# A cast moved to ScalarE and a mask product cut in two at the start of a fused retention and MLP kernel

## The chip, the cores and the metric

The kernel runs on one core of one Trainium2 chip. The metric is the device time of one execution in microseconds (us), the median of several runs. The measured time is some 1.8 us longer than the span that the profile shows (214.87 against 213.1 us for the profiled run of the kernel before).

## The reference

A recurrent retention layer over 4 batches, 8 heads, 768 steps and a head size of 64, then a layer norm and an MLP (512 to 2048 to 512) with a residual:

```python
for t in range(S):
    state = gamma[None, :, None, None] * state + np.einsum('bhd,bhe->bhde', k[:, :, t], v[:, :, t])
    y[:, :, t] = scale * np.einsum('bhd,bhde->bhe', q[:, :, t], state)
...
mu, var = x.mean(-1), ((x - mu) ** 2).mean(-1)          # shortened
xn = (x - mu) / np.sqrt(var + 1e-06) * g_ln
out = x + np.maximum(xn @ w_ch1, 0.0) @ w_ch2
```

## The kernel before

The 768 steps are cut into chunks of 128, which gives 24 tiles of 128 rows. For each tile TensorE transposes k and q (tasks tk and tq), VectorE scales the transposed q (trq), TensorE multiplies q and k (pa), VectorE applies the decay mask (asb), TensorE multiplies with v (py, and pyS for the part that comes from the state; pd updates the state), VectorE takes the statistics and normalizes (xn), TensorE transposes (tx), ScalarE copies the result (xnt), and then come the MLP units (m1, with a relu by ScalarE or VectorE) and the second product (m2). For the first eight tiles an MLP unit is 16 matmuls, 0.89 us: one tile with one of the four chunks of w1.

The order of all this is not written down. Tasks are listed with an engine (or a choice of engines), an estimated duration, a rank and what they wait for; a planner in the kernel simulates them and fixes the order of each engine's instructions before the program is built. So a change of one entry can move instructions anywhere.

```python
def order(self):
    ...
    key = at + t["polite"], t["rank"], at      # the task that can start first, then by rank
    if best is None or key < best[0]:
        best = key, t, e
...
def c_mask(eng):
    nc.vector.tensor_tensor(
        out=mask, in0=vsc[:, 0, :].unsqueeze(2).to_broadcast([P, H, P]),
        in1=cm.unsqueeze(1).to_broadcast([P, H, P]), op=ALU.mult)
...
maskd = a(DVE, 1230, -50, c_mask, [vscd, tri])
...
# tile 0: loaded as fp32 by two hardware queues, and cast; the other tiles are cast by GpSimd's DMA
raw = a(ACT if kind == "q" else SP, 390, -200 + "kqv".index(kind), emit32, (),
        ("osb", kind), (), 0, {"k": 3400, "q": 4000, "v": 4800}[kind])
loaded[kind, j] = a({"k": {ACT: 620}, "q": {DVE: 490}, "v": {ACT: 620, DVE: 430}}[kind], 0, -60, emit,
                    [raw], takes, [("osb", kind)])
...
tk = a(PE, 230, r - 0.1, e_tk, [loaded["k", t], ident] + ([tq] if tq else []),
       ("tp", ("k", t)), [where["k", t]], follows=[pat] if t == 1 else [])
...
m = a(PE, 865, 500 + unit["1", g, ho], e_m1,
      [ex[t] for t in range(G0[g], G0[g] + n)] + [loaded["w1", ho // 4]],
      ("mm", key), [("xnt", hb)])
```

The loads after tile 0 are issued by GpSimd one after another: k, q and v of the next tiles with the chunks of w1 between them, then w2.

## Time and profile before

| | before |
|---|---|
| time, median of 3 | 214.69 us (214.67 to 214.78) |
| span in the profile | 213.1 us |
| TensorE busy | 203.6 us, 96% |
| VectorE, GpSimd, ScalarE busy | 57%, 42%, 38% |
| TensorE starts tk of tile 4, the seam | 23.39 us |
| TensorE ends its last matmul | 210.02 us |

From the page of the kernel before, the busy time of each engine and TensorE's share of 40 equal slices in tenths (9 is 90% or more):

```profile
PE 203.6 (96%) x1935; PEld 131.4 (62%) x1955; DVE 121.3 (57%) x235; ACT 80.8 (38%) x152; POOL 89.8 (42%) x105
...
PE   7769999999999999999999999999999999999994
```

The row of digits says where most of the idle time lies: in the first three slices (16 us), where TensorE waits for loads and for the chain of the first tiles, and in the last one. It says so roughly. The busy time holds 6.4 us of filler, matmuls on zeros (L650) that the planner puts into early gaps, so the early slices wait longer than their digits say; and a 9 can hide up to a tenth of 5.3 us, as in the fifth slice the wait of 0.44 us at the seam. From the start of tk4 at the seam to its last end TensorE is busy in 185.40 of 186.63 us, so after the seam there is nearly nothing to gain by a faster engine alone, while anything that makes TensorE wait there is felt.

### The profile page before, as it was taken

The numbers are of one execution on the slowest core, as the hardware profiler recorded it, in microseconds if no ns is written. First come the engines' busy times: TensorE is split into PE (matmuls) and PEld (weight loads), VectorE is DVE, ScalarE is ACT, GpSimd is POOL, SyncE is SP. The second block draws the span as 40 slices with busy tenths as digits, with TensorE's granted clock in tenths as the row PEclk, the third lists the DMA queues.
The fourth block names the chain that finished last, engine by engine and source line by source line (L and its number), as shares of the span: only waits on it lengthen the run. The fifth ranks groups of instructions, "written<-read, shape, count | busy, mean of one in ns | idle before, by whom it ended". The sixth has DMA issues, their size and how long they took to land.

```text
span 213.1 us, 4678 instructions
## 1 busy us (share of the span) xinstructions
PE 203.6 (96%) x1935; PEld 131.4 (62%) x1955; DVE 121.3 (57%) x235; ACT 80.8 (38%) x152; POOL 89.8 (42%) x105
## 2 busy tenths in 40 slices
PE   7769999999999999999999999999999999999994
PEld 2448899995476556777877785454544444444442
DVE  7688778961736989987872869793511111012121
ACT  4446655772042203645644353145640044430000
POOL 8988699826498395665834550000000000000000
PEclk9999999999999999999999999999999999999999
DMA  7999999999999999999999999820121111011212
GB/s 140 180 179 180 180 156 190 169 185 155 149 202 190 130 245 201 134 165 128 172 131 142 122 177 152 222 77 0 34 65 50 52 49 49 0 52 49 98 49 98
DMA packets 109382, 27.17 MB, mean 127 GB/s; under 512 B 102065, under 2 KB 106417, under 8 KB 109362
## 3 DMA queue, kind: packets, MB, share of 16 engines
q0 software_dynamic: 75984, 13.24, 87.8%
q1 hardware_dynamic: 32194, 13.31, 34.7%
q10 hardware_dynamic: 1184, 0.33, 0.7%
q8 instruction: 15, 0.25, 0.5%
q14 instruction: 5, 0.04, 0.1%
HBM read 27.27 MB, written 6.29 MB: 157 GB/s over the span
## 4 chain that ended last, share of the span: by engine, by line
PE 87%; DMA 8%; POOL 2%; issue 1%; DVE 0%; POOLq 0%
PE tp L626 39%; PE mm L589 37%; DMA ksb<-in_k_dram 5%; DMA w<-in_moe_w_ch_dram 3%; PE pa L443 3%; PE pd L512 2%; PE py L466 2%; PE py L462 2%; PE tp L542 1%; POOL k L342 0%; PE tp L403 0%; POOL qsb L342 0%; POOL v L342 0%; POOL w L350 0%; PE tp L411 0%
## 5 line engine op out<-in xcount | busy, mean ns | idle before, releaser
L589 PE MATMUL mm<-xnt,w 128*128 128x128 bf16 (+2 forms) x896 | 93.7, 257 | 0.0
L626 PE MATMUL tp<-w,h 128*128 128x512 bf16 (+2 forms) x381 | 86.7, 370 | 1.2 <-issue 0.3
L602 ACT ACTIVATE h<-mm 128x512 bf16<-128x512 f32 x88 | 52.5, 597 | 70.5 <-PE mm L589 59.6
L589 PEld LDWEIGHTS <-w 128*128 128x128 bf16 x896 | 65.7, 98 | 18.5
L626 PEld LDWEIGHTS <-h 128*128 128x128 bf16 x400 | 37.3, 98 | 38.8
L634 DVE SCALAR_TENSOR_TENSOR osb<-tp,rstd,x_all 128x512 f32<-128x512 f32 (+2 forms) x25 | 18.2, 728 | 55.3 <-PE tp L626 55.1
L450 DVE TENSOR_TENSOR asb<-pa,mask 128x1024 bf16<-128x1024 f32 x24 | 29.3, 1220 | 9.6 <-PE pa L443 9.4
L480 DVE BATCH_NORM_STATS2 bns<-py 128x6 f32<-128x512 f32 x24 | 16.7, 696 | 14.6 <-PE py L466 14.4
L499 POOL TENSOR_TENSOR vg<-vsb,vsc 128x512 bf16<-128x512 bf16 x16 | 17.2, 1073 | 13.3 <-DMA vsb<-in_v_dram 9.2
L486 ACT CAST x_all<-py 128x512 bf16<-128x512 f32 x24 | 14.0, 583 | 19.1 <-DVE xn L475 19.0
L342 POOL DMA_DIRECT2D qk<-in_k_dram x17 | 15.2, 893 | 12.3 <-DMA tr<-qk 9.9
L342 POOL DMA_DIRECT2D vsb<-in_v_dram x20 | 18.5, 923 | 1.2 <-DMA w<-in_moe_w_ch_dram 0.8
L475 DVE SCALAR_TENSOR_TENSOR xn<-py,mv,gb 128x512 bf16<-128x512 f32 x24 | 18.0, 751 | 0.9
L526 DVE TENSOR_TENSOR state<-pd,gch 64x256 bf16<-64x256 f32 x40 | 16.7, 417 | 0.3
L342 POOL DMA_DIRECT2D qk<-in_q_dram x17 | 15.2, 894 | 3.4 <-DMA w<-in_moe_w_ch_dram 3.4
L433 DVE TENSOR_TENSOR trq<-tr,qsc 128x512 bf16<-128x512 bf16 x17 | 7.9, 463 | 2.9 <-DMA tr<-qk 2.9
L564 ACT ACTIVATE rstd<-mv,epsb 128x1 f32<-128x1 f32 (+2 forms) x14 | 3.7, 289 | 11.8 <-DVE mv L481 11.8
L466 PEld LDWEIGHTS <-asb 128*128 128x128 bf16 x192 | 7.8, 98 | 0.3 <-DVE trq L416 0.3
L462 PEld LDWEIGHTS <-trq 128*128 128x128 bf16 x80 | 6.0, 98 | 3.2
L466 PE MATMUL py<-vsb,asb 128*128 128x64 bf16 x160 | 7.9, 193 | 0.0
L462 PE MATMUL py<-state,trq 128*128 128x128 bf16 x80 | 7.7, 219 | 0.1
L650 PE MATMUL mm<-zeros 128*128 128x512 bf16 (+1 forms) x24 | 6.4, 394 | 1.4 <-DVE zeros L221 1.2
(65 smaller groups left out, 108.4 us busy)
## 6 DMA issues: line engine op xcount, KB each, us to landing
out_dram<-osb SPq DMA_DIRECT2D x23, 256.0 KB, 4.0
w<-in_moe_w_ch_dram POOLq DMA_DIRECT2D x8, 512.0 KB, 10.3
vsb<-in_v_dram POOLq DMA_DIRECT2D x20, 128.0 KB, 8.8
qk<-in_k_dram POOLq DMA_DIRECT2D x17, 128.0 KB, 9.3
qk<-in_q_dram POOLq DMA_DIRECT2D x17, 128.0 KB, 9.9
qsb<-in_q_dram POOLq DMA_DIRECT2D x6, 128.0 KB, 8.7
k<-in_k_dram POOLq DMA_DIRECT2D x3, 128.0 KB, 7.4
v<-in_v_dram POOLq DMA_DIRECT2D x3, 128.0 KB, 9.0
```

Of the source, the lines that this page charges most:

```text
L342: nc.gpsimd.dma_start(out=tile_of(kind, j), in_=src)
L450: nc.vector.tensor_tensor(out=take("asb", t, [P, NPAIR, 2, P], BF16).rearrange("p i a t -> p a i t"), in0=held["pa", t], in1=mask.rearrang ...
L462: nc.tensor.matmul(py[:, 2 * i:2 * i + 2, :], lhsT=held["trq", t][:, i, :], rhs=held["pb", t][:, i, :], start=(mi == 0), stop=False)
L466: nc.tensor.matmul(py[:, h, :], lhsT=held["asb", t][:, h // 2, h % 2, :], rhs=tile_of("v", t)[:, h, :], start=(mi == 0), stop=(mi == n - 1))
L475: nc.vector.scalar_tensor_tensor(out=take("xn", t, [P, DM], BF16), in0=held["py", t].rearrange("p h d -> p (h d)"), scalar=mv[:, t, 0:1], ...
L480: nc.vector.bn_stats(out=bns[:, t, :], in_=held["py", t].rearrange("p h d -> p (h d)"))
L499: e.tensor_tensor(out=take("vg", j, [P, H, D], BF16), in0=tile_of("v", j), in1=vsc[:, cc, :].unsqueeze(2).to_broadcast([P, H, D]), op=ALU. ...
L526: nc.vector.tensor_tensor(out=held["pb", n][o, :, o], in0=held["pd", b][o, :, o], in1=gch[o, cc, :].unsqueeze(2).to_broadcast([D, NPAIR, D ...
L589: nc.tensor.matmul(p[:, j, :], lhsT=w1[:, ko, (ho + j) * P:(ho + j + 1) * P], rhs=held["xnt", hb][:, h0:h0 + n, ko, :], start=(ko == 0), s ...
L602: nc.scalar.activation(out=dst, in_=src, func=AF.Relu)
L626: nc.tensor.matmul(held[key], lhsT=held["h1", hb][:, ho, i * P:(i + 1) * P], rhs=w2[:, ho, cols], start=(ho == 0), stop=(ho == HO - 1))
L634: nc.vector.scalar_tensor_tensor(out=take("osb", key, [P, w], FP32), in0=held[key], scalar=rstd[:, t:t + 1], in1=x_all[:, t, cols], op0=AL ...
```

## The change

Its intent is to shorten the start. The cast of v goes to ScalarE, which is idle then (from 6.62 to 8.46 us in the trace before), so VectorE is free for the first scaled q; and the mask product is cut into two halves of heads, so the first half runs while q is still on its way. Estimates of landing times and of the setup were adjusted with it, for the planner.

```diff
-    def c_mask(eng):
+    def c_mask(eng, s):
+        n = s.stop - s.start
         nc.vector.tensor_tensor(
-            out=mask, in0=vsc[:, 0, :].unsqueeze(2).to_broadcast([P, H, P]),
-            in1=cm.unsqueeze(1).to_broadcast([P, H, P]), op=ALU.mult)
+            out=mask[:, s], in0=vsc[:, 0, s].unsqueeze(2).to_broadcast([P, n, P]),
+            in1=cm.unsqueeze(1).to_broadcast([P, n, P]), op=ALU.mult)
...
-    small = a(DVE, 1450, -100, c_small)
+    small = a(DVE, 1550, -100, c_small)
...
-    maskd = a(DVE, 1230, -50, c_mask, [vscd, tri])
+    maskd = a(DVE, 640, -50, lambda eng: c_mask(eng, slice(0, H // 2)), [vscd, tri])
+    maskd = a(DVE, 640, -45, lambda eng: c_mask(eng, slice(H // 2, H)), [maskd], at=5300)
...
-                        ("osb", kind), (), 0, {"k": 3400, "q": 4000, "v": 4800}[kind])
+                        ("osb", kind), (), 0, {"k": 3400, "q": 3800, "v": 5200}[kind])
...
-                loaded[kind, j] = a({..., "v": {ACT: 620, DVE: 430}}[kind], 0, -60, emit,
+                loaded[kind, j] = a({..., "v": {ACT: 620}}[kind], 0, -60, emit,
```

More of the change, by code (lines that the diff above doesn't have):

```diff
@@ L334, in emit @@
                              held["osb", kind].rearrange("p (h d) -> p h d", d=D))
-                loaded[kind, j] = a({"k": {ACT: 620}, "q": {DVE: 490}, "v": {ACT: 620, DVE: 430}}[kind], 0, -60, emit,
+                loaded[kind, j] = a({"k": {ACT: 620}, "q": {DVE: 490}, "v": {ACT: 620}}[kind], 0, -60, emit,
                                     [raw], takes, [("osb", kind)])
```

## The prediction

General statements that no run of this case shows are cut from the text below, at the marked places: on how the engines' queues run, on formulas for the time of an operation, on small DMA packets, on loads that no engine can hasten and on transposes behind stores. The times the forecast uses (1.23, 0.68 and 0.62 us) are read from the trace, and its sum came to +0.7, 215.4, of which 215.3 was taken. In the trace of the kernel before the stretches from 8 to 40 us move 156 to 206 GB/s, a little wider than the 174 to 206 said below.

> **What bounds the kernel now.** I read the page's busy shares first, then the chain of work that ended last, then the stretches, then the timeline of the first 44 us. TensorE is busy 96% of 213.1 us at full clock; nothing else is over 57%. The chain says where the other 4% lies:
>
> ```profile
> 4.19 7.25 DMA w<-in_moe_w_ch_dram
> ...
> 11.73 0.76 POOL w L350
> 12.66 10.68 DMA ksb<-in_k_dram
> 23.39 0.40 PE tp L403 x4
> 23.78 0.89 PE mm L589 x16
> ...
> 197.95 12.09 PE tp L626 x71
> 210.06 0.35 DVE osb L634
> ```
>
> Columns: start, length, what. Up to 23.39 us the chain is DMA: loads by GpSimd, one after another, down to k of tile 4 (the L403 transpose is "tk4" below; tasks are numbered in their order on TensorE). From 23.39 on it is TensorE alone, to 210.06. The stretches (length, busy us with counts for TensorE, its weight loads, VectorE, ScalarE, GpSimd; clock, DMA share, GB/s) say the same:
>
> ```profile
> 20.00:24.00 4.00, 3.14 (x59) 2.92 (x59) 3.29 (x8) 1.70 (x4) 1.91 (x4) 1.00 1.99 174
> 24.00:28.00 4.00, 4.00 (x76) 3.79 (x73) 2.52 (x4) 2.72 (x5) 3.73 (x5) 1.00 1.82 180
> 36.00:40.00 4.00, 4.00 (x78) 4.00 (x77) 3.88 (x8) 2.05 (x4) 4.00 (x5) 1.00 1.24 206
> 40.00:44.00 4.00, 4.00 (x76) 4.00 (x74) 3.46 (x8) 3.40 (x8) 2.19 (x3) 1.00 1.33 153
> ```
>
> The last idle time of TensorE before it fills up is this wait, at the seam:
>
> ```profile
> 22.55 0.40 PE L466 MATMUL py<-v,asb 128*128 128x64 bf16 x8
> 23.39 0.40 PE L403 MATMUL tp<-idn,ksb 128*128 128x128 bf16 x4 [0.44 <-DMA ksb<-in_k_dram]
> ```
>
> So the end is 23.39 (landing of k of tile 4) + 186.6 us of gapless TensorE work + 3.1 us of tail. What is done sooner ahead of 23.39 gains only if it takes TensorE work across that seam; what stalls TensorE after it costs in full.
>
> [...] matmuls behind the k transposes waited too, though their weights (the chunk issued at 11.73) landed at about 22.4. So the order of instructions, which this change moves, decides who waits. [...] here the mask takes 1.23 us and a 128x512 fp32 product (L243) 0.68. [...] here k's cast takes 0.62. [...] the early stretches move 174 to 206 GB/s without a pause. [...]
>
> **The change, part by part.** The built kernel has the same instructions but for one mask product more and one cast moved; the planner in the kernel gives another order on TensorE, VectorE and ScalarE. GpSimd's order is the same, so I take the load landings as unchanged.
>
> *Start, VectorE.* Now:
>
> ```profile
> 5.60 0.49 DVE L188 CAST qsb<-osb 128x512 bf16<-128x512 f32 x1
> 6.88 0.43 DVE L188 CAST v<-osb 128x512 bf16<-128x512 f32 x1 [0.79 <-DMA osb<-in_v_dram]
> 7.22 0.42 DVE L416 TENSOR_TENSOR trq<-tp,qsc 128x512 bf16<-128x512 bf16 x1
> ```
>
> The first half of the mask runs 4.36 to 5.04 (0.68). The q cast does not come sooner: q lands at 5.58 (issue 0.74 + 4.8). The second half takes 6.02 to 6.70, which is where VectorE idled for v; the split costs 2 x 0.68 - 1.23 = 0.13 us of VectorE, hidden. v's cast goes to ScalarE, idle between 6.62 and 8.46: 6.88 to 7.50, needed at 8.9. So the first trq starts at about 6.62, 0.6 sooner: pa0 7.1, first asb ends about 8.8 (now 9.36).
>
> *To the first MLP matmuls.* The gain matrix product (1.08 us, L295) now stands ahead of tq1 rather than after it, py0 directly behind: py0 at 9.2 (now 9.91); statistics behind the second trq from 9.75 (10.34); xn0 ends 11.5 (12.12); its transpose 11.57 (12.18); its copy on ScalarE ends 12.7 (13.29); first MLP unit m1#1 at 13.05 (now 13.70). 0.65 us gained so far.
>
> *It goes again before the seam.* The new order puts m1#1 ahead of tq2 (now 13.23, then about 13.93), and VectorE takes statistics and xn of tile 1 ahead of trq2: trq2 14.86 to 15.29 (now 13.66 to 14.09), so pa2 15.34 (14.69), asb2 ends 17.0 (16.83). py2 then stands behind two MLP units and starts about 17.5 (16.89), xn2 ends 19.65 (19.03), its copy 20.8 (20.38), m1#5 and m1#6 follow, py3 about 22.6 (now 22.55). tk4 waits for its DMA until 23.39, with some 0.5 us to spare. In both orders exactly the same work stands ahead of tk4 (four tk, tq, pa and py, three tx, one pd, six m1 units). Value of the early part: 0.0.
>
> *After the seam* the work is the same, in another order. Two places look tight.
> (a) tk5 moves from behind py4 to behind m1#10. With today's spacings TensorE gets there at 27.40 + 0.89 = 28.29; k of tile 5 lands at 18.03 + 10.4 = 28.4. Stall: about 0.2 us.
> (b) pd3 and one more m1 unit go ahead of py5, so VectorE starts the chain from py5 1.1 us later relative to TensorE's work than now. That chain is dense already:
>
> ```profile
> 35.66 0.70 DVE L480 BATCH_NORM_STATS2 bns<-py 128x6 f32<-128x512 f32 x1 [0.53 <-PE py L466]
> ...
> 36.60 0.75 DVE L475 SCALAR_TENSOR_TENSOR xn<-py,mv,gb 128x512 bf16<-128x512 f32 x1
> 37.27 1.22 DVE L450 TENSOR_TENSOR asb<-pa,mask 128x1024 bf16<-128x1024 f32 x1
> 38.40 0.85 DVE L526 TENSOR_TENSOR state<-pd,gch 64x256 bf16<-64x256 f32 x2
> 39.28 0.69 DVE L604 TENSOR_SCALAR h<-mm 128x512 bf16<-128x512 f32 x1
> 39.89 0.69 DVE L480 BATCH_NORM_STATS2 bns<-py 128x6 f32<-128x512 f32 x1
> ```
>
> The new order keeps this run and puts the relu of m1#20 between the last statistics and xn6. mm has two buffers, so m1#22 waits for that relu. From py5's start: statistics after 0.44 (35.66 - 35.22), the run to the second statistics 4.23 (39.89 - 35.66), 0.93 for them with the aggregate, 0.69 relu: 6.3 us. TensorE from py5 to m1#22: py5 0.33, pa6 0.33, two m1 1.79, tx5 0.22, m1 0.90, pyS and py6 0.45, two m1 1.79: 5.8 us. Stall: about 0.5 us, not made up later, since TensorE has no idle time to give back.
> Later orders move by a unit or two; the w2 chunks (the last lands near 49.0, needed near 52) and the transposed tiles have over a microsecond of slack where I checked.
>
> Sum: 214.69 - 0.0 + 0.2 + 0.5 = 215.4; I take 215.3, since (b) rests on some twelve steps added up and may be hidden in part.
>
> **Rivals.** *The early gain reaches the end* (0.6 us off, 214.1): for it, the first 14 us do get shorter by my own sum; against it, the wait on the DMA at 23.39 and equal work ahead of it. *Nothing moves at all* (214.7): k5 lands 0.2 us sooner, or VectorE's gaps make up for (b); quite possible. *A new wait further on* (216 or more): the order of DMA transposes and stores on the sync queue changes too[...]; against it, the first twelve tiles that I walked through have slack. *The early chain misses the seam*: every step of tile 1 to 3 would have to take some 0.1 us longer than I add up, so that py3 slips by over 0.5 us; from there on each further 0.1 us is lost at the end (215.5 to 216).
>
> **Range and chances.** Every term is under 1 us and 2% is 4.3 us. Low end: no stall and a little luck, 214.4; high end: both stalls and one more like (b), 216.3. Faster by over 2% would need the DMA stream to shorten by 4 us: 1%. Slower by over 2% would need a stall chain of 4 us: 2%.
>
> **What would show it.** Right: first trq at about 6.6, m1#1 at about 13.05, yet tk4 again at 23.4 with a DMA as the releaser and a longer idle time or an equal one before it; a short idle at tk5 (about 28.4); an idle of some 0.5 us ahead of an MLP unit near 42 released by VectorE's relu; otherwise TensorE full to the end. Wrong: tk4 well before 23.3 (the stream can be hastened), no idle near 42 (VectorE has more slack than I add up), or new idle times of TensorE after 50 us.

## The result, and the profile after

The changed kernel takes 215.46 us (median of 4 runs, 215.31 to 215.51) against 214.74 for the kernel before, run alongside (median of 4 runs, 214.67 to 214.97). The ratio is 1.0031 with a 95% interval of 1.0013 to 1.0048: within 2%, and slower. (A ratio here is the mean time of one kernel's fast runs over that of the other's in the same rounds, so it is not quite the ratio of the medians quoted.) The predicted 215.3 and the range of 214.4 to 216.3 hold.

The start went as meant. VectorE's timeline after the change (start, length, engine, line, operation, what was written from what, shapes; in brackets the idle time before it and what ended that):

```profile
4.35 0.69 DVE L263 TENSOR_TENSOR mask<-vsc,cm 128x512 f32<-128x512 f32 x1
5.57 0.51 DVE L188 CAST qsb<-osb 128x512 bf16<-128x512 f32 x1 [0.53 <-DMA osb<-in_q_dram]
6.00 0.67 DVE L263 TENSOR_TENSOR mask<-vsc,cm 128x512 f32<-128x512 f32 x1
6.64 0.42 DVE L419 TENSOR_TENSOR trq<-tp,qsc 128x512 bf16<-128x512 bf16 x1
```

The q cast still waits for its load (5.57 now, 5.60 before), the second half of the mask (6.00 to 6.67) fills what was idle time (0.79 us ahead of the cast of v), and the first trq starts at 6.64 instead of 7.22. The two halves together take 1.36 us, where the whole took 1.23. (An operation of VectorE can begin in these records before the one ahead of it ends: the q cast ends at 5.57 + 0.51 = 6.08, and the mask's second half starts at 6.00. So durations added up come out too long by up to 0.09 us for each operation in the dense runs shown here.)

The gain holds until the first MLP unit (13.06, before 13.70). Of these 0.64 us 0.13 are left at the seam. The rest goes where one more task (tq of tile 2, 0.2 us) now lies behind the first unit, and where TensorE waits more than before (1.46 us up to the seam instead of 1.11 up to the wait there), in two new places for ScalarE's copies of xn. TensorE's timeline after the change:

```profile
16.04 1.95 PE L592 MATMUL mm<-xnt,w 128*128 128x128 bf16 x32 [0.37 <-ACT xnt L188]
...
21.12 2.06 PE L592 MATMUL mm<-xnt,w 128*128 128x128 bf16 x32 [0.37 <-ACT xnt L188]
```

Its later part holds the seam and the first of the new waits (L406 is the transpose of k, L592 an MLP unit):

```profile
23.02 0.40 PE L469 MATMUL py<-v,asb 128*128 128x64 bf16 x8
23.26 0.39 PE L406 MATMUL tp<-idn,ksb 128*128 128x128 bf16 x4
...
27.27 1.06 PE L592 MATMUL mm<-xnt,w 128*128 128x128 bf16 x16
28.70 0.40 PE L406 MATMUL tp<-idn,ksb 128*128 128x128 bf16 x4 [0.37 <-DMA ksb<-in_k_dram]
```

The task tk4 at 23.26 follows py3 without any wait on a DMA: k of tile 4 had landed at 22.98 (23.34 before), and TensorE itself came late. The wait on a DMA is at tk5 now, on k of tile 5, which landed at 28.65. The chain that ended last (start, length, what) has moved accordingly: what was a load up to 23.34 before is now the next tile's load, and further on VectorE is in it, which is not so before the change:

```profile
17.94 10.71 DMA ksb<-in_k_dram
28.65 0.05 issue
28.70 0.40 PE tp L406 x4
...
41.50 0.62 DVE bns L483
42.12 0.02 issue
42.14 0.18 DVE mv L484
42.32 0.59 DVE h L607
42.91 0.04 issue
42.95 1.05 PE mm L592 x16
```

The last line is the 22nd MLP unit, which waits for the relu of the 20th (h, L607), and that relu stands behind statistics in VectorE's queue. The table of stretches shows the same in total. The row of 24 to 30 us before (length, then busy us of TensorE with its count, weight loads, VectorE, ScalarE, GpSimd; clock, DMA share, GB/s):

```profile
24.00:30.00 6.00, 6.00 (x116) 5.79 (x113) 3.93 (x7) 3.91 (x7) 5.62 (x7) 1.00 2.03 171
```

and after:

```profile
24.00:30.00 6.00, 5.63 (x102) 5.25 (x100) 4.09 (x8) 3.87 (x7) 5.15 (x7) 1.00 2.07 171
30.00:44.00 14.00, 13.78 (x259) 13.29 (x257) 12.06 (x23) 8.81 (x18) 12.31 (x14) 1.00 1.59 179
```

TensorE was full in both stretches before (the 36 to 44 us rows in the prediction show two of them). Now 0.37 and 0.22 us are idle. TensorE's last matmul ends at 210.64, 0.61 later than before (from unrounded times).

Measured by start times the waits are a little larger than the idle time shown, since a matmul's record reaches past the start of the next one (the unit at 27.27 has a record of 1.06 us). An MLP unit takes 0.89 us from start to start, so tk5 would have begun at 27.27 + 0.89 = 28.16 and began 0.54 later; for the 22nd unit, the tasks from py5 on add up to 5.82 and it began 6.20 after py5 (42.95 - 36.75), 0.38 later. The balance of the first trace is then: seam -0.13, tk5 +0.54, 22nd unit +0.38, and -0.18 over the remaining 167 us in changes of 0.05 to 0.2 us at borders between kinds of matmuls, which I did not resolve; the sum is +0.61.

One thing I had not seen in the prediction showed when I listed which tile and which chunk of w1 each MLP unit uses, instead of numbering the units by position (t is the tile, c the chunk of w1):

```
slot     1    2    3    4    5    6    7    8    9    10   11   12   13
before  t0c0 t0c1 t1c0 t1c1 t2c0 t2c1 t0c2 t1c2 t2c2 t3c0 t0c3 t1c3 t2c3
after   t0c0 t1c0 t0c1 t1c1 t2c0 t0c2 t1c2 t2c1 t2c2 t0c3 t1c3 t2c3 t3c0
```

The units changed places as well. Slot 2 now takes tile 1, so it waits for tile 1's copy (the wait at 16.04). And the last chunk of w1 (c3) is used for the first time in slot 10, at 27.27, instead of slot 11, at 28.30. It landed at 27.16 in this trace, with 0.1 us to spare.

### The profile page after: what moved, and what is told of

It reads as the page before. It is cut to its first block, busy times and chain, and to the rows that moved or that the text cites. A ratio compares the mean times of both kernels' runs of the same rounds, so it can differ in the third digit from the quotient of the medians.

```text
span 213.7 us, 4675 instructions
## 1 busy us (share of the span) xinstructions
PE 204.1 (96%) x1934; PEld 131.9 (62%) x1955; DVE 119.6 (56%) x234; ACT 82.4 (39%) x154; POOL 89.3 (42%) x105
## 3 DMA queue, kind: packets, MB, share of 16 engines
HBM read 27.27 MB, written 6.29 MB: 157 GB/s over the span
## 4 chain that ended last, share of the span: by engine, by line
PE 75%; DMA 8%; DVE 8%; POOL 4%; issue 2%; POOLq 0%
PE mm L592 34%; PE tp L629 33%; DMA ksb<-in_k_dram 5%; DMA w<-in_moe_w_ch_dram 3%; PE pa L446 2%; DVE asb L453 2%; PE py L469 2%; PE py L465 2%; PE pd L515 2%; DVE bns L483 2%; DVE state L529 1%; DVE osb L637 1%; POOL qsb L345 1%; POOL w L353 1%; DVE h L607 1%
## 5 line engine op out<-in xcount | busy, mean ns | idle before, releaser
L592 PE MATMUL mm<-xnt,w 128*128 128x128 bf16 (+2 forms) x896 | 94.5, 257 | 1.0 <-ACT xnt L188 0.7
L605 ACT ACTIVATE h<-mm 128x512 bf16<-128x512 f32 x89 | 53.1, 597 | 77.7 <-PE mm L592 66.6
L592 PEld LDWEIGHTS <-w 128*128 128x128 bf16 x896 | 65.9, 98 | 21.2 <-issue 1.0
L436 DVE TENSOR_TENSOR trq<-tr,qsc 128x512 bf16<-128x512 bf16 x17 | 7.2, 425 | 0.1
```

Of the source, the lines that this page charges most:

```text
L592: nc.tensor.matmul(p[:, j, :], lhsT=w1[:, ko, (ho + j) * P:(ho + j + 1) * P], rhs=held["xnt", hb][:, h0:h0 + n, ko, :], start=(ko == 0), s ...
L605: nc.scalar.activation(out=dst, in_=src, func=AF.Relu)
```

## The experiments

The kernels differ from one of the two by an edit of the planner's entries or of its finished list, as the snippets show. In them `seq` is the planner's list, `named` finds a task by kind and tile, `units` are the MLP units in order of slots, `ek` and `eq` are the evictions that belong to tk and tq, and `behind(x, y)` moves x to the place right after y. "Last end" is the end of TensorE's last matmul in the trace (210.02 before, 210.64 after). Every result was correct.

### ops_old_order: the new operations in the old order

The planner runs on the old entries, and only what is emitted changes: the cast, and the mask product in two halves back to back, both ahead of the q cast (in the changed kernel the q cast lies between them). This separates the cost of the operations from that of the order.

```diff
+        for s in (slice(0, H // 2), slice(H // 2, H)):      # in c_mask: two halves, back to back
+            nc.vector.tensor_tensor(out=mask[:, s], ...)
...
+    seq = plan.order()
+    loaded["v", 0]["eng"] = ACT
```

> The operations of the change (v of tile 0 cast by ScalarE, mask product in two halves, both ahead of the q cast) in the instruction order of the kernel before. Order theory: the operations cost nothing where they lie, the first trq starts about 6.7 us, the tile-4 k transpose (tk4) is again held at its landing near 23.0 to 23.4, TensorE is gapless after it, time 214.7 (ratio 1.000 +-0.001). Rival, the operations themselves cost time (0.13 us more VectorE, 0.62 us more ScalarE): 215.4, as the changed kernel.

Measured: 214.84 us, ratio 0.9986 (0.9959 to 1.0014), last end 210.16. TensorE's timeline at the seam:

```profile
22.43 0.40 PE L470 MATMUL py<-v,asb 128*128 128x64 bf16 x8
23.14 0.40 PE L407 MATMUL tp<-idn,ksb 128*128 128x128 bf16 x4 [0.31 <-DMA ksb<-in_k_dram]
```

In the old order the seam is again a wait on the load, which landed at 23.09, and there is no wait after it until 114 us. The operations are free here, within the noise: the interval leaves room for 0.3 us of cost, and the ratio is low in part because one of the eleven runs of the kernel before took 216.6 (the medians are 214.84 and 214.85; the same run lowers the ratios of tk5_back, tk5_only and relu20_act, which by medians are 1.0033, 1.0041 and 1.0031). So what costs is the order that the planner makes of them, by elimination: no run has the new order with the old operations. The 0.25 us by which the seam came sooner was lost again near 131 us, and 0.14 more, where products of VectorE (trq) took longer than elsewhere; more of that below.

The trace also shows where the early gain of the change comes from. The first trq starts at 6.65 here, as early as after the change, but TensorE's timeline gains little by it:

```profile
8.74 0.40 PE L415 MATMUL tp<-idn,qsb 128*128 128x128 bf16 x4 [0.51 <-DMA qsb<-in_q_dram]
8.97 1.08 PE L299 MATMUL mm<-grow,ones 128*128 128x512 f32 x2
...
9.94 0.40 PE L470 MATMUL py<-v,asb 128*128 128x64 bf16 x8
...
13.59 0.78 PE L593 MATMUL mm<-xnt,w 128*128 128x128 bf16 x11
```

TensorE waits for q of tile 1, the gain matrix product (L299) stands behind that, py0 starts at 9.94 (9.91 before) and the first MLP unit at 13.59 (13.70 before). In the changed kernel the gain matrix product stands ahead of tq1 (8.03 and 8.95) and fills this wait. So of the 0.64 us of early gain about 0.1 comes with the operations alone, and the rest needs the new order.

### tk5_back and tk5_only: tk5 put back behind py4

The first asks the planner for it, which then rearranges other things too; the second only moves the two tasks in the finished list.

```diff
# tk5_back
-                   follows=[pat] if t == 1 else [])
+                   follows=[pat] if t == 1 else [pyt] if t == 5 else [])
# tk5_only
+    behind(named["tk", 5], named["py", 4])
+    behind(named["ek", 5], named["tk", 5])
```

> The changed kernel, with one more planning constraint: tk5 not before py4. The planner then returns to the order of before from tk4 on to the MLP unit 21. Order theory: both waits go (0.54 us at tk5 and 0.39 us at the 22nd MLP unit), tk4 stays near 23.26, time 214.5 to 214.7 (ratio 0.999). Rival, the early part or the operations are what costs: 215.4 as the changed kernel.

> The changed kernel with only tk5 and its eviction put behind py4 in the finished order, all else as changed. Order theory: 0.54 us less, the wait near 42.7 stays: 214.9 to 215.0 (ratio 1.001). Rival, the wait on the load is hidden or only moves to the next instruction (tq5 is then held for its own load): 215.4 to 215.5.

Measured: tk5_back 215.56 us, ratio 1.0019 (0.9992 to 1.0045), last end 210.78; tk5_only 215.73 us, ratio 1.0029 (1.0004 to 1.0055), last end 210.96. Both expectations missed. The wait at tk5 was gone, and another stood one task ahead of it. TensorE's timeline of tk5_back:

```profile
27.07 0.40 PE L515 MATMUL pd<-vg,ksb 128*128 128x128 bf16 x4
28.14 1.24 PE L592 MATMUL mm<-xnt,w 128*128 128x128 bf16 x19 [0.67 <-DMA w<-in_moe_w_ch_dram]
```

The last chunk of w1 landed at 28.09 here and at 27.82 in tk5_only, after 27.16 in the first trace of the changed kernel. So slot 10 waited 0.67 and 0.50 us, more than the 0.37 us of idle time at tk5. My theory that the wait at tk5 was the whole cost of this place fell. Two loads come in one behind the other here (28.09 and 28.83 in tk5_back, 27.82 and 28.64 in tk5_only), and the new order needs the first of them one slot too early and the second one task too early.

### relu20_act: the relu of the 20th unit to ScalarE

This takes away what the 22nd unit waited for.

```diff
+    r20["eng"] = ACT               # r20: the relu of units[19]
```

> The changed kernel with the relu of the 20th MLP unit on ScalarE instead of VectorE, all else as changed; tk5 still early. Order theory: the idle time near 42.7 goes, 0.39 us less, the wait at tk5 stays: 215.05 to 215.1 (ratio 1.0016). Rival, TensorE is held by something else there (xn of tile 6, the table load of ScalarE): the idle time moves to the next instruction and the time stays 215.4 to 215.5.

Measured: 215.52 us, ratio 1.0022 (0.9997 to 1.0047), last end 210.73. TensorE's timeline:

```profile
28.14 1.07 PE L595 MATMUL mm<-xnt,w 128*128 128x128 bf16 x16 [0.88 <-DMA w<-in_moe_w_ch_dram]
...
41.11 2.98 PE L595 MATMUL mm<-xnt,w 128*128 128x128 bf16 x48
```

The 20th to 22nd units run as one block of 48 matmuls, without the idle time; the table load of ScalarE, which the rival names, takes 1.28 us from 40.91 on. Aligned by start times against the changed kernel, TensorE stood 0.33 us later before this place and 0.09 later after it: 0.25 of the 0.38 us was gained, and the rest came back ahead of the next transpose (43.93, where it could have begun at 43.79). The expectation of 215.05 to 215.1 missed: this execution, too, had the late chunk (28.09) and lost 0.88 us at slot 10. Against the second trace of the changed kernel below, which has the same late chunk, its last end is 0.24 sooner (210.73 and 210.97).

### units_only, units_tk5, units_tk5_relu: the parts undone one after another

The unit of tile 3 goes back into slot 10 (the same four units in slots 10 to 13, relu engines as in the changed kernel); then tk5 goes back as well; then the relu goes to ScalarE as well.

```diff
+    reorder(units[9:13], [units[12]] + units[9:12])       # all three
+    behind(named["tk", 5], named["py", 4])                # units_tk5, units_tk5_relu
+    behind(named["ek", 5], named["tk", 5])
+    relu_of[id(units[19])]["eng"] = ACT                   # units_tk5_relu
```

> The changed kernel with the first MLP unit of tile 3 (it needs no new load) put into the 10th slot again, ahead of the first unit on the last w1 chunk, as in the kernel before; tk5 stays early. New theory (two landings are walls in the changed order: the last w1 chunk, landed at 27.2 to 28.1 us in the runs so far, and k of tile 5, at 28.4 to 29.0, and either alone costs about as much as both): TensorE no longer waits ahead of the 10th unit, but 0.4 to 0.8 us at tk5 instead; time as the changed kernel, ratio 1.002 to 1.003. Rival (the last w1 chunk is the only wall): ratio 1.000 to 1.001.

> The same, and tk5 and its eviction put behind py4: both walls are out of the way. New theory: no idle time of TensorE from 23.3 to 42, the wait of about 0.25 us for VectorE's relu near 42.7 stays, TensorE is done 0.5 us sooner than in the changed kernel, ratio 1.0005 to 1.001. Rival (the new order costs at other places, or the early part does): ratio stays 1.002 to 1.003.

> The same, and the relu of the 20th MLP unit on ScalarE: all three waits are out of the way. New theory: TensorE gapless from 23.3 us on, done about 0.1 us sooner than in the kernel before (tk4 starts about 23.25 instead of 23.39), ratio 0.999 to 1.000. Rival as for the run above.

Measured: units_only 215.91 us, ratio 1.0051 (1.0038 to 1.0064), last end 210.94; units_tk5 215.37 us, 1.0032 (1.0016 to 1.0048), 210.56; units_tk5_relu 215.37 us, 1.0020 (1.0006 to 1.0033), 209.91. TensorE's timeline of units_only:

```profile
27.41 1.06 PE L595 MATMUL mm<-xnt,w 128*128 128x128 bf16 x16
28.68 0.40 PE L406 MATMUL tp<-idn,ksb 128*128 128x128 bf16 x4 [0.21 <-DMA ksb<-in_k_dram]
```

With a unit in slot 10 that doesn't need the chunk, TensorE goes through to tk5 and waits there for k of tile 5: undoing one of the two moves alone gains nothing, as tk5_only and tk5_back had shown from the other side. The wait came as expected, though smaller (0.21 us idle, 0.38 by start times, where 0.4 to 0.8 was expected), and the ratio lies above the 1.002 to 1.003 expected. With both undone (units_tk5) there is no wait from the seam to 42 us, although the chunk landed at 28.12, late again: slot 11 takes it at 28.27. With the relu moved too, the trace has no idle time of TensorE of 0.1 us or more from 23 us to the end, and the profiled run took 214.78 us, like the kernel before. Part of that is its start: k of tile 4 landed at 22.75 in this execution, and tk4 came at 23.00 instead of 23.26.

The times agree only in part. units_tk5 was to be closer to the kernel before than it was: its last end is 0.08 us sooner than the changed kernel's, where I had expected 0.5 (it had the late chunk; against the second trace of the changed kernel, which had it too, it is 0.41 sooner). By start times of the same matmuls it reached the seam 0.11 later, gained the 0.54 at tk5, and then lost 0.08 at tq5, 0.08 at the pd at 32.03 and 0.18 at the pd at 35.33, which starts 0.41 after the tq ahead of it and 0.23 after it in the changed kernel. Short waits took the place of the long one. And of the five runs of units_tk5_relu the profiled one is the fastest; the others took 215.20 to 215.59. No trace of a slow one exists, so where they lose 0.4 to 0.8 us is open.

The traces can be compared without their starts, from the start of tk4 to TensorE's last end: 186.64 us before, 187.38 and 187.73 in the two traces of the changed kernel, 187.54 with the units alone put back, 187.19 with tk5 too, 186.91 with the relu too. So undoing the three moves takes back 0.47 to 0.82 of the 0.74 to 1.09 us that the new order costs after the seam, in one traced execution; 0.27 stay, and so does what the median of units_tk5_relu (ratio 1.0020) shows beyond it.

### after_again: the changed kernel a second time

It is the same program, run and traced once more, to see whether the first trace was typical.

> The changed kernel once more, unaltered, for a second trace and for timing in the same session. Landing theory: the last w1 chunk lands anywhere from 27.1 to 28.1 us; if it lands after 27.2 TensorE waits ahead of the 10th MLP unit instead of (or besides) at tk5, and the end stays within 0.3 us of the first trace; ratio 1.002 to 1.003. Rival (the waits of the first trace are fixed by the program): the same idle times at the same places, 0.37 us ahead of tk5.

Measured: 215.82 us (215.49 to 216.05), ratio 1.0044 (1.0032 to 1.0057), last end 210.97. The chain that ended last:

```profile
17.17 10.92 DMA w<-in_moe_w_ch_dram
28.09 0.05 issue
28.14 1.07 PE mm L592 x16
29.20 0.22 PE tp L406 x4
```

The same program lost its time in another place, as expected, though the ratio is above the 1.002 to 1.003 expected: the chunk landed at 28.09 instead of 27.16, slot 10 waited (28.14, in place of 27.27), and tk5 behind it did not wait any more. From slot 10 to before tk5 TensorE stood 0.87 us later than in the first trace, from tk5 on only 0.33 later. The two waits do not add: whichever comes first hides most of the other. Of the five traces with the chunk's first use in slot 10 and the whole change (the changed kernel twice, tk5_back, tk5_only, relu20_act) only the first has the early chunk, the one from which I would have explained everything by tk5.

### cast_alone: the first part of the change by itself

```diff
-                loaded[kind, j] = a({..., "v": {ACT: 620, DVE: 430}}[kind], 0, -60, emit,
+                loaded[kind, j] = a({..., "v": {ACT: 620}}[kind], 0, -60, emit,
```

> One part of the change alone: v of tile 0 cast by ScalarE alone, the mask product in one piece and all planning times as before. The planner then puts the first unit on the last w1 chunk in the 10th slot and tk5 ahead of the 11th, as with the whole change. Order theory: ratio 1.002 to 1.003, with idle time ahead of the 10th unit or tk5. Rival (splitting the mask, or the altered planning times, is what matters): ratio 1.000.

Measured: 215.40 us, ratio 1.0029 (1.0017 to 1.0042), last end 210.97. The planner gives slot 10 to t0c3 and puts tk5 early, as with the whole change. It is not the same order throughout: slot 2 keeps t0c1, as before. In this trace the chunk landed at 27.41 and k of tile 5 at 28.36, so neither place cost much, and there is the wait of the 22nd unit. There are also waits of 0.2 to 0.6 us at three places between 18.8 and 22.3 us, but they do not count against the kernel before, since tk4 still comes at 23.35. From 43 to 93 us TensorE is even 0.18 ahead of the first trace of the changed kernel; about half of the 0.95 us by which it ends later than the kernel before was lost near 93 and 97 us, where one trq of VectorE took 2.12 us, and the traced run is the slowest of the five (215.80; the others took 215.33 to 215.49). One entry of the planner is enough to bring most of the new order and a ratio of the same size, but this trace does not show that the same waits make it up.

### old_swap: the old order with slots 10 and 11 swapped

Only the early use of the last chunk of w1, put into the kernel before.

```diff
+    reorder(units[9:11], [units[10], units[9]])
```

> The kernel before, unchanged in its operations and its order but for one swap: the first unit on the last w1 chunk takes the 10th MLP slot and the first unit of tile 3 the 11th, as the changed kernel has it. New theory: TensorE waits ahead of the 10th unit for that chunk, landing + 0.05 - 27.40, so 0.2 us (landing 27.5) to 0.7 us (28.1), and the end moves by that: ratio 1.001 to 1.0035. Rival (the order of the units does not matter; the operations of the change do): ratio 1.000, no idle time there.

Measured: 215.14 us, ratio 1.0012 (0.9998 to 1.0025), inconclusive. In the traced run the chunk landed at 27.25, so there was hardly a wait (slot 10 started at 27.30 and could have at 27.18), and that run took 214.66. The expectation (a wait of 0.2 us or more) missed there. The six runs fall into two groups, 214.66 to 214.88 and 215.39 to 215.40. That is what one would see if the chunk came late in half of them, but only the one was traced, so it is not shown.

### seam_old_ops and seam_new_ops: the wait at the seam filled

If the order decides, the wait at 23.39 us in the kernel before can be filled: let one more MLP unit go ahead of tk4, and one more ahead of tq4. seam_new_ops does the same with the operations of the change in the old order.

```diff
+    behind(named["tk", 4], units[6])
+    behind(named["ek", 4], named["tk", 4])
+    behind(named["tq", 4], units[7])
+    behind(named["eq", 4], named["tq", 4])
```

> The kernel before with one edit of the order: tk4 goes behind the 7th MLP unit (whose w1 chunk has landed 0.9 us sooner than k of tile 4) and tq4 behind the 8th. Order theory: the idle time of 0.3 to 0.44 us at the seam is filled, every later instruction of TensorE starts 0.3 to 0.5 us sooner unless the last w1 chunk (28.1 at the latest) holds the 11th unit, now reached at 27.8: ratio 0.998 (0.997 to 0.9995). Rival (the landing of k of tile 4 is a wall for the whole block): ratio 1.000.

> The same edit with the operations of the change (cast on ScalarE, mask in two halves ahead of the q cast) in the order of before. Order theory: as the run with the old operations, ratio 0.998 (0.997 to 0.9995), since the operations are free where they lie; this would beat both kernels. Rival (operations cost, or the landing is a wall): 1.000 or more.

Measured: seam_old_ops **214.50 us**, ratio 0.9980 (0.9968 to 0.9993), last end 209.53; seam_new_ops 214.81 us, ratio 0.9991 (0.9978 to 1.0005), last end 210.03. TensorE's timeline of seam_old_ops:

```profile
22.31 0.40 PE L470 MATMUL py<-v,asb 128*128 128x64 bf16 x8
22.54 1.06 PE L595 MATMUL mm<-xnt,w 128*128 128x128 bf16 x16
23.44 0.39 PE L406 MATMUL tp<-idn,ksb 128*128 128x128 bf16 x4
...
99.47 0.40 PE L447 MATMUL pa<-trq,tr 64*128 64x128 bf16 x8
```

There is no wait at the seam: the unit fills it, and tk4 comes when its load has long landed. From about 25.6 us on TensorE is 0.73 to 0.85 us ahead of the kernel before; 0.23 of that was there at the first MLP unit already (13.46, before 13.70), as this execution's loads came sooner (tq1, which waits for q of tile 1, started at 8.48, before 8.70). It keeps 0.50: 0.24 are lost ahead of the pa at 99.47. That pa waits for VectorE's scaled q of its tile, and this product was slow:

```profile
98.37 1.04 DVE L437 TENSOR_TENSOR trq<-tr,qsc 128x512 bf16<-128x512 bf16 x1
```

Elsewhere the same operation mostly takes 0.42 us (the median of the 17 in the trace before). Its input, a tile transposed by DMA, had landed at 94.38, so the DMA was not what held it. Over the fourteen traces 20 of 336 such products took 0.7 us or more, and all 20 ran at least in part beside a product of GpSimd's (vg). That goes together; no run tests whether one causes the other, and some products of 0.42 us ran beside a vg too. The losses near 131 us in ops_old_order and near 93 us in cast_alone stand at such products. The two traces of the changed kernel hold none of them, so they do not explain its loss.

seam_old_ops is faster than both others, though by 0.2% only. seam_new_ops missed its expectation: its interval includes 1, so it shows no gain. In its trace 0.40 us were lost at the same place (a trq of 1.30 us), and its first MLP unit started at 13.52: the earlier trq of the change brought no earlier start in the old order.

### Landings in all traces

The time at which the last chunk of w1 landed, and the start of the nearest packet of the DMA queue of the kind "instruction" (called the fetch here), in us:

```
                 fetch    chunk 3 of w1   k of tile 5   waited there
before           24.86    27.53           28.44         -
ops_old_order    24.84    27.56           28.46         -
seam_old_ops     24.62    27.18           28.10         -
seam_new_ops     24.74    27.47           28.37         -
old_swap         24.66    27.25           28.21         -
cast_alone       24.96    27.41           28.36         -
after            25.73    27.16           28.65         tk5
units_only       25.82    27.30           28.63         tk5
after_again      25.90    28.09           28.87         slot 10
tk5_back         25.89    28.09           28.83         slot 10
tk5_only         25.63    27.82           28.64         slot 10
relu20_act       25.70    28.09           28.98         slot 10
units_tk5        25.89    28.12           28.97         -
units_tk5_relu   25.48    27.73           28.59         -
```

In all six traces with the fetch before 25 us the chunk landed by 27.56, and in six of the eight with a later fetch it landed at 27.7 or later. The order alone does not set the time of the fetch: cast_alone has most of the new order and fetched at 24.96. In every trace 14 of the 16 completion marks of this load were in by 26.70, and only the last one or two came later (after 26.54 comes 27.16 in the first trace of the changed kernel, after 26.57 comes 28.09 in the second). So one or two of its 16 parts came late, not the whole load. The DMA view of the changed kernel from 24 to 29 us (queue and kind: packets, MB, share of the 16 engines' span) has this packet:

```profile
q0 software_dynamic: 4076, 0.86, 197.3%
q8 instruction: 1, 0.02, 1.2%
```

It is one of 15 of 16 KB in the whole profile. It took 1.2% of 16 x 5 us, and the packet's own record has 0.94 us, which is the size of the difference seen (27.16 against 28.09). But no run moved the fetch alone, and two traces with a late fetch had an early chunk, so it is not shown that the fetch sets the landing back.

## Why the prediction was right, and where it was not

**What bounds the kernel.** Right in the main. TensorE was nearly full after the seam before the change (185.40 of 186.63 us), and of the 0.79 us by which the two new waits and the seam set it back (-0.13 + 0.54 + 0.38) 0.61 was left at the end. ("Nothing else is over 57%" overlooks the weight loads, 62% on the page; they belong to TensorE's own work.)

**The start.** Right, within 0.03 us: first trq 6.62 predicted and 6.64 measured, py0 9.2 and 9.17, m1#1 13.05 and 13.06. The prediction took 0.68 us for a half of the mask, from a product of the same size in the trace; the halves took 0.69 and 0.67. ops_old_order shows that these operations cost nothing beyond the noise by themselves, and that they gain little by themselves too: py0 came at 9.94 there. Most of the early gain needs the other thing that the prediction names, the gain matrix product ahead of tq1.

**"It goes again before the seam", value 0.0.** Right that the gain is lost; the reason given was wrong, and the value was -0.13. I had said that tk4 waits for its DMA until 23.39 with 0.5 us to spare. Two things failed. "I take the load landings as unchanged": k of tile 4 landed 0.36 sooner (22.98). Over the fourteen traces it landed between 22.75 and 23.34, and in the old order too it came at 23.09 (ops_old_order), so this need not be the change's doing. And py3 came at 23.02, not 22.6, since two MLP units waited 0.37 us each for copies by ScalarE, the first of them because slot 2 now holds another tile's unit. So TensorE itself set the time, 23.26. The rival "the early chain misses the seam" was half true: py3 slipped, by 0.4 us.

**(a) tk5, 0.2.** Right in its mechanism for the first trace, with the term too small: 0.54, as TensorE came 0.13 sooner and k of tile 5 landed 0.25 later than I took. It is not the whole of that place, though. tk5_only, tk5_back and units_only show a second load, the last chunk of w1, that was needed one slot sooner; after_again shows that its wait often takes the place of the one at tk5. **The step that failed is "Later orders move by a unit or two"**, with m1 units numbered by position: two orders that look alike by number held different units in slots 2 and 10.

**(b) the 22nd unit, 0.5.** Right in its mechanism, with the releaser named (VectorE's relu), and 0.38 by start times. VectorE's run was 0.15 us shorter than my sum; the tasks of TensorE added up to 5.82, as said. relu20_act took the wait away and gained 0.25; units_tk5_relu against units_tk5, from tk4 on, 0.28.

**The sum.** +0.7 by the terms (215.4, of which I took 215.3); the trace has +0.61, the two sessions have +0.72 and +1.04. That the number fell so well is partly luck: in the first trace -0.13 at the seam, 0.12 too much at the 22nd unit and -0.18 later on made up for 0.34 too little at tk5, and in the second session the loss at slot 10 was larger.

**The rivals.** "The early gain reaches the end" is refuted in this order. "Nothing moves at all" is refuted by both intervals, which lie above 1. The "new wait further on" came, not from the transposes by DMA but from a load of weights, and it took the place of the wait at tk5 rather than being added to it.

**What stays open:** why the same load lands 0.9 us apart in two executions of one program; the 0.27 us and the slower runs of units_tk5_relu, so what the new order costs beside the three named waits; and what makes the trq of VectorE slow in the waits near 93, 99, 116 and 131 us, which come and go between executions.

## What to carry to other kernels

Where a planner decides the order, compare the orders by what each slot needs (which tile, which weights), not by positions; a small gain at the start can reorder the whole program, and the order cost some 0.7 to 1.0 us here, by elimination, while the operations were free within 0.3 us. A wait for a load on a full engine is worth filling with other ready work, which gained more here (0.998) than making the work ahead of it faster (1.0031). The same load of the same program landed at 27.16 and at 28.09 us in two executions, so a slack of less than 0.9 us was not safe here. Trace the same program twice before a wait of half a microsecond is called the cause.
